# Block-causal attention into a squared-ReLU MLP: row maxima that scale the scores in PSUM, 32-bit moves of k's halves, and weight bits prepared on GpSimd

## The chip, the core and the metric

The kernel runs on one core of one Trainium2 chip. A core has five engines with a queue of instructions each: TensorE (PE in the profile, with its weight loads as PEld), VectorE (DVE), ScalarE (ACT), GpSimd (POOL) and SyncE (SP), whose queue issues the transfers between the chip's memory and SBUF. PE writes its results to PSUM, DVE and ACT read and write PSUM and SBUF, GpSimd works on SBUF. The metric is device time in microseconds, as the median of the runs; a lower time is better.

## The reference

```python
# q, k, v: 8 batches, 8 heads, 576 positions, 64 per head; blocks of 64 positions
scores = scale * np.matmul(q, k.transpose(0, 1, 3, 2))
scores = np.where(block_i >= block_j, scores, -1000000000.0)
scores = scores - np.max(scores, axis=-1, keepdims=True)
attn = np.exp(scores)
attn = attn / (np.sum(attn, axis=-1, keepdims=True) + 1e-09)
x = np.matmul(attn, v)            # then 4608 rows of 512
h = x @ w_in                      # 512 -> 2048
r = np.maximum(h, 0.0)
out = (r * r) @ w_out             # 2048 -> 512
```

The mask works on blocks: a row of block j sees the 64(j+1) positions of blocks 0 to j, so the kernel computes scores of 64 to 576 columns for the nine blocks of rows. The two weight matrices come as float64 numbers, which the kernel reads as pairs of 32-bit words.

## The kernel before, in words

**Attention passes.** Two heads are done together in a pass, one in each half of the partitions; eight batches of four pairs make 32 pairs. The first two batches are split by rows: passes 0 to 7 do row blocks 0 to 2 (G_X), passes 8 to 15 blocks 3 to 8 (G_Y). Passes 16 to 39 do all nine blocks of the other six batches (G_XY). Passes below 16 are "native": their scores are fp32 matmuls (L422). Passes below 12 are "whole": their weights are turned by PE (L515) and multiplied with fp32 v (L547). The others split every fp32 number into a high and a low fp16 part (`front`, L395 and L398 make the low parts of k and q, L402 makes `k2`, which is `k1` with its high and low halves exchanged), turn them by DMA transposes and multiply in fp16 (L433).

**Softmax of a group.** A pass has its row blocks in groups of two to four; a group's scores lie in one PSUM tile `ps` of two banks. For each block DVE takes the negated maximum of the row (L457), then one instruction multiplies the group's maxima by the scale `es` (L460), a constant in native passes and a [128, 1] tile in the others. ACT computes exp(es * score + nmx) from PSUM and its sum (L463), GpSimd adds 1e-9 to the sums (L471), DVE inverts them (L472), and ACT and DVE write the two fp16 parts of the weights, `p_rows` (L487, L488). DMA turns these (L491), PE multiplies with v (L547), ACT reads that out (L554).

**The MLP.** Its rows are taken in 12 chunks of 384 (`moe_in`, `moe_out`). A chunk is 16 hidden steps of 12 matmuls each (L683, followed by Relu on ACT L689, the square L691, and the two fp16 parts on DVE L692 and L693) and 12 output steps of 12 matmuls (L708, read out by DVE in L715). The weights are needed as two fp16 parts. `weight_scale` finds their largest value (L257), `weight_parts` makes the parts: ACT computes fp32 words from the high word of each float64 (L295), DVE shifts them by 3 (L296) and puts in the top 3 bits of the low word (L297), ACT casts to the high part (L298), DVE subtracts to get the low one (L299). w_in is loaded once, at the start (`load_w1`), into buffers that partly lie in the still unused w_out tiles; w_out is loaded twice (`load_w`, L217), for its scale and for its parts, through three buffers and eight free stretches of the w_out tiles (SPARE).

**The order of the work.** `one_pass` issues a pass; between its groups `pour` issues MLP steps, FILL[i // 4 - 2] of them in pass i, from the list of chunks that are ready. What is left when the passes end is issued after them. The first chunk goes through `first_moe`, which mixes its hidden steps with the rest of w_in's parts, w_out's scale (two pieces a step from step 2 on) and w_out's parts: PTN = 3 a step from step PT0 on, where PT0 = 16 means behind all hidden steps. The program is built with scheduling on (`schedule_with_timeline_sim`): an instruction may be placed on its engine's queue earlier or later than the code has it, as a planner finds its inputs ready, but the queues are fixed when the program runs. On PE, ACT, DVE and GpSimd an instruction that waits holds up all behind it.

Of the kernel before, what the change touches and what calls it, by code (L numbers as in the profile page):

```python
# [8 lines left out]
F32 = mybir.dt.float32  # L9
F16 = mybir.dt.float16  # L10
BF16 = mybir.dt.bfloat16
I32 = mybir.dt.int32
I64 = mybir.dt.int64
AF = mybir.ActivationFunctionType
ALU = mybir.AluOpType
AX = mybir.AxisListType
PSUM = bass.MemoryType.PSUM

P = 128
D = 64  # L20
# [9 lines left out]
A_ATT = 14  # L30
# [10 lines left out]
SC0 = 2  # L41
SCN = 2
PTN = 3
PT0 = 16
X_POOL = 1
QF = (6, 7)
WT = 1
# [1 line left out]
SPARE = {0: 2, 1: 3, 2: 4, 3: 5, 4: 6, 5: 7, 8: 6, 9: 7}  # L49
# [15 lines left out]
NW = -1  # L65
XR_ACT = 1
DELAY = (14, 6, 1)
FILL = (14, 5, 7, 7, 10, 10, 8, 7)

# [28 lines left out]
def attention_moe_kernel(ctx: ExitStack, tc: tile.TileContext, qkt, qk, vm, vt, w_in, w_out, out):  # L100
    nc = tc.nc
# [9 lines left out]

    one = const.tile([1, 1], F32, name="one")
    nc.vector.memset(one, 1.0)
    ones_bf = const.tile([P, P], BF16, name="ones_bf")
    nc.vector.memset(ones_bf, 1.0)

# [87 lines left out]
    def words(raw):  # L204

        w = raw.bitcast(I32).rearrange("p (n t) -> p n t", t=2)
        wf = raw.bitcast(F32).rearrange("p (n t) -> p n t", t=2)
        return w[:, :, 0], w[:, :, 1], wf[:, :, 1]

    def spare(k):  # L210

# [3 lines left out]
    def load_w(src, f, name, at=None):  # L215
        raw = p2.tile([P, 512], I64, tag="qk32", name=name, bufs=3) if at is None else spare(at)
        nc.sync.dma_start(raw, src[f])  # L217
        return words(raw)
# [10 lines left out]
    w1raw = []  # L229
# [5 lines left out]
    def load_w1(f, pool):  # L235


        if f in QF:
            raw = p2.tile([P, 512], I64, tag="qk32", name=f"w1raw{f}", bufs=3)
        elif f < 8:  # L240
            raw = pool.tile([P, 512], I64, name=f"w1raw{f}")
        else:
            w = (w2h, w2l)[f // 12].rearrange("p f d -> p (f d)").bitcast(I64)
            raw = w[:, f % 4 * 512 : f % 4 * 512 + 512]
        nc.sync.dma_start(raw, w_in[f])
        w1raw.append(words(raw))

    def weight_scale(wi):

        tok, ng = ((tokA, NG), (tokB, 1))[wi]
        st = small.tile([P, NF], F32, tag="stw", name=f"stw_{wi}", bufs=1)
        n = NF // ng
        for f in range(NF):
            _, _, hf = load_w(w_out, f, f"wa{wi}_{f}") if wi else w1raw[f]
            i = nc.vector.tensor_reduce(st[:, f : f + 1], hf, axis=AX.X, op=ALU.max, apply_absolute_value=True)  # L257
            if wi == 0 and f >= BS and (1, 0) in gate:
                behind(i, gate[1, 0])
            if f % n == n - 1:  # L260
                q = f // n
                st1 = small.tile([P, 1], F32, tag="st1", name=f"st1_{wi}_{q}", bufs=1)
                nc.vector.reduce_max(st1, st[:, f + 1 - n : f + 1], axis=AX.X)
                m = pow2_of_max(st1, 1, f"w{wi}_{q}", 2.0**-27, wm[:, q : q + 1] if wi == 0 else None)
                s = wsc[wi][:, q : q + 1]
                nc.vector.tensor_scalar(
                    s.bitcast(I32), m.bitcast(I32), -1, (127 + 64 + W_TOP) << 23, op0=ALU.mult, op1=ALU.add
                )
            yield
        if wi == 0:  # L270
            m = small.tile([P, 1], F32, tag="m", name="m_w")
            nc.vector.reduce_max(m, wm, axis=AX.X)
        nc.vector.tensor_scalar(
            tok.bitcast(I32), m.bitcast(I32), 8, (127 - W_EXP) << 23, op0=ALU.mult, op1=ALU.add
        )
        if wi == 0:
            nc.vector.tensor_scalar(tokA, tokA, 2.0 ** (A_X + A_W - 1), None, op0=ALU.mult)
            inv = scale_of(m, 0, 1, "w")
            nc.vector.tensor_scalar(wm, wm, inv, None, op0=ALU.mult)
            nc.vector.tensor_tensor(wm, wm, wm, op=ALU.mult)  # L280
        else:
            nc.vector.tensor_scalar(tokB, tokB, tokA, None, op0=ALU.mult)
            nc.vector.tensor_scalar(wm, wm, wsc[1], None, op0=ALU.mult)

    def weight_parts(wi):

        wh, wl = ((w1h, w1l), (w2h, w2l))[wi]
        for f in range(NF):
            wlo, whi, hf = load_w(w_out, f, f"wb{wi}_{f}", SPARE.get(f)) if wi else w1raw[f]
            if WT:  # L290
                t = p1.tile([P, 512], F32, tag=("qs", "k1", "k2")[(wi + f) % 3], name=f"wt{wi}_{f}")
            else:
                t = p2.tile([P, 512], F32, tag="r", name=f"wt{wi}_{f}", bufs=3)
            q = f * NG // NF
            nc.scalar.activation(t, hf, AF.Prelu, scale=(wm if wi else wsc[0])[:, q : q + 1], alpha=-(2.0**32))  # L295
            nc.vector.tensor_scalar(whi, t.bitcast(I32), 3, None, op0=ALU.logical_shift_left)  # L296
            nc.vector.scalar_tensor_tensor(whi, wlo, 29, whi, op0=ALU.logical_shift_right, op1=ALU.bitwise_or)  # L297
            nc.scalar.copy(wh[:, f], hf)  # L298
            nc.vector.tensor_tensor(wl[:, f], hf, wh[:, f], op=ALU.subtract)  # L299
            yield  # L300
# [3 lines left out]
    def load_first(b, hp):  # L304

        n = NHP // 2 * b + hp // 2
# [13 lines left out]
        for c in range(2):  # L320
            o = v[:, c, 0:4].rearrange("p (h n) d -> p h n d", h=2)
            nc.sync.dma_start(o, vm[b, hp + c, :, :, 0:2, :])
            passes[NHP * b + hp + c].update(
                qz=[t[:, c, h] for h in range(2)], kf=t[:, c, 2], chunks=2, v32=o, es=D**-0.5
            )

    def load(t):
# [31 lines left out]
    def front(t):  # L359

        u, c = t["u"], t["chunks"]
        if t["whole"]:
            t["es"] = D**-0.5
            return
        v32 = t["v32"][:, :, 0:c, :]
        st = small.tile([P, 3], F32, tag="st", name=f"st_{u}")
# [17 lines left out]
        nc.vector.tensor_scalar(xsc, m[:, 2 - a : 3 - a], 2.0 ** (-A_ATT - A_P), None, op0=ALU.mult)  # L384
        t["xsc"] = xsc
        if t["native"]:
            t["es"] = D**-0.5
        else:
            es = t["es"] = small.tile([P, 1], F32, tag="es", name=f"es_{u}")
            nc.vector.tensor_scalar(  # L390
                es, m[:, 0:1], m[:, 1:2], 2.0 ** (-2 * A_ATT) * D**-0.5, op0=ALU.mult, op1=ALU.mult
            )
            nc.scalar.activation(k1[:, :, 0:D], k3, AF.Copy, scale=s[:, 1:2])
            nc.scalar.activation(qs[:, :, 0:D], q3, AF.Copy, scale=s[:, 0:1])
# [3 lines left out]
            nc.vector.scalar_tensor_tensor(  # L398
                qs[:, :, D:P], q3, s[:, 0:1], qs[:, :, 0:D], op0=ALU.mult, op1=ALU.subtract
            )  # L400
            halves = k1.rearrange("p j (z d) -> p j z d", z=2)
            nc.vector.tensor_copy(k2.rearrange("p j (z d) -> p j z d", z=2), halves[:, :, ::-1, :])  # L402
            qT = t["qT"] = p2.tile([P, NJ, P], F16, tag="qT", name=f"qT_{u}")
            kT = t["kT"] = p2.tile([P, 2, NJ, P], F16, tag="kT", name=f"kT_{u}")
            nc.sync.dma_start_transpose(kT[:, 0], k1.rearrange("p j d -> p (j d)"))
# [36 lines left out]
    def softmax(t, group, complete):  # L442
# [11 lines left out]
            scores(t, ps, j, off)  # L454
        for i, (j, off) in enumerate(group):
            w = D * (j + 1)
            nc.vector.tensor_reduce(  # L457
                nmx[:, i : i + 1], ps[:, off : off + w], axis=AX.X, op=ALU.max, negate=True
            )
        nc.vector.tensor_scalar(nmx, nmx, es, None, op0=ALU.mult)  # L460
        for i, (j, off) in enumerate(group):
            w = D * (j + 1)
            nc.scalar.activation(  # L463
                p32[:, off : off + w],
                ps[:, off : off + w],
                AF.Exp,
                bias=nmx[:, i : i + 1],
                scale=es,
                accum_out=sm[:, i : i + 1],
            )  # L470
        nc.gpsimd.tensor_scalar(sm, sm, 1e-9, 2.0**-A_P, op0=ALU.add, op1=ALU.mult)  # L471
# [429 lines left out]
```

## Time and profile before

| | us |
|---|---|
| median of 3 runs | 1070.2 |
| lowest and highest of them | 1069.17 and 1070.45 |
| the profiled execution | 1070.82 |
| span of its core, first instruction to last | 1069.0 |

In the profiled execution the mean granted clock of PE is 0.981 of full speed, and the transfers move 133.08 MB at a mean of 124 GB/s.

In the rows of the profile, a group stands as: line, engine, operation, output<-input by the program's names, shapes, xcount | busy us, mean ns of one | idle us of the engine just before them <-what ended it. PE's rows are of pipelined matmuls: one row's time is longer than the distance to the next matmul, so the distance is read from start times or from a long piece of the chain. A wait row reads: who waited, for what, total us, times, longest.

### The profile page before, as it was taken

What the parts mean: (1) busy time and instruction counts of PE and PEld (TensorE: products, weight loads), DVE (VectorE), ACT (ScalarE), POOL (GpSimd) and SP (SyncE); (2) the same over time, 40 slices, a digit from 0 to 9 for tenths busy, and PEclk for the clock granted to TensorE, in tenths of its full rate; (3) what the DMA queues carried; (4) which work ended last, traced back from release to release, by engine and by line L of the source; (5) the groups of instructions that cost most, each with busy time, mean ns of one, the idle gap of its engine ahead of it and who ended that gap; (6) DMA issues with size and microseconds to landing.
All of it is one profiled execution on the core that took longest, in us unless ns stands there. A gap on an engine that the chain in (4) does not pass through costs nothing.

```text
span 1069.0 us, 18806 instructions
## 1 busy us (share of the span) xinstructions
PE 1008.9 (94%) x6836; PEld 537.2 (50%) x6836; DVE 708.9 (66%) x1859; ACT 681.2 (64%) x1668; POOL 49.5 (5%) x151
## 2 busy tenths in 40 slices
PE   6789889999988998999999999999999999999998
PEld 4345434544544454555445455455445545455553
DVE  5999787777777678968569469768967334232230
ACT  6697875885897589669559469669857315032230
POOL 2010110000000000000001000000100000000000
PEclk9799989999999998999999999999999999999999
DMA  8777259687867677769456667767574220000000
GB/s 274 260 251 270 64 169 225 121 156 151 183 136 138 139 139 152 148 133 164 116 118 129 138 134 135 147 148 129 107 142 78 31 62 1 20 11 11 21 1 29
DMA packets 303900, 133.08 MB, mean 124 GB/s; under 512 B 275648, under 2 KB 288960, under 8 KB 303808
## 3 DMA queue, kind: packets, MB, share of 16 engines
q1 hardware_dynamic: 303808, 131.90, 55.2%
q8 instruction: 53, 0.87, 0.3%
q14 instruction: 39, 0.32, 0.1%
HBM read 55.31 MB, written 9.44 MB: 61 GB/s over the span
## 4 chain that ended last, share of the span: by engine, by line
PE 60%; ACT 8%; DVE 8%; DMA 7%; issue 4%; SPq 1%; POOL 0%; ACTq 0%; DVEq 0%; POOLq 0%
PE po L708 33%; PE ph L683 19%; PE ps L433 4%; PE px L547 3%; ACT p L463 2%; ACT p_rows L487 2%; DMA kT<-k 2%; DMA p_turned<-p_rows 2%; DMA qT<-qs 2%; DVE nmx L457 2%; DVE p_rows L488 2%; ACT r L689 1%; ACT r L691 1%; DMA vraw<-in_vt 1%; DVE g L693 1%
## 5 line engine op out<-in xcount | busy, mean ns | idle before, releaser
L683 PE MATMUL ph<-xt,w1h 128*128 128x384 f16 x1536 | 378.5, 329 | 14.6 <-ACT r L689 13.7
L708 PE MATMUL po<-w2h,g 128*128 128x512 f16 x1152 | 355.3, 382 | 3.0 <-ACT w2h L298 2.0
L708 PEld LDWEIGHTS <-g 128*128 128x128 f16 x1728 | 165.7, 98 | 205.1 <-issue 17.9
L683 PE MATMUL ph<-xt,w1l 128*128 128x384 f16 x768 | 251.8, 328 | 0.0
L708 PE MATMUL po<-w2l,g 128*128 128x512 f16 x576 | 220.1, 382 | 2.2 <-DVE w2l L299 2.1
L683 PEld LDWEIGHTS <-w1h 128*128 128x128 f16 x1536 | 145.0, 98 | 122.3 <-issue 32.9
L689 ACT ACTIVATE r<-ph 128x384 f32<-128x384 f32 x192 | 93.3, 494 | 137.0 <-PE ph L683 135.4
L463 ACT ACTIVATE p<-ps,nmx,es 128x320 f32<-128x320 f32 (+8 forms) x216 | 131.6, 621 | 68.7 <-DVE nmx L460 60.4
L457 DVE TENSOR_REDUCE nmx<-ps 128x1 f32<-128x192 f32 (+8 forms) x288 | 125.4, 481 | 50.3 <-PE ps L433 40.2
L488 DVE SCALAR_TENSOR_TENSOR p_rows<-p,rs,p_rows 128x384 f16<-128x384 f32 (+4 forms) x264 | 128.0, 523 | 28.6 <-ACT p_rows L487 26.4
L487 ACT ACTIVATE p_rows<-p,rs 128x384 f16<-128x384 f32 (+4 forms) x264 | 124.6, 549 | 14.5 <-DVE rs L472 8.2
L715 DVE TENSOR_SCALAR ob<-po,uv 128x512 f32<-128x512 f32 x36 | 29.0, 807 | 122.9 <-PE po L708 122.8
L692 DVE CAST g<-r 128x384 f16<-128x384 f32 x192 | 66.9, 353 | 64.5 <-ACT r L691 64.2
L693 DVE TENSOR_TENSOR g<-r,g 128x384 f16<-128x384 f32 x192 | 104.8, 552 | 2.8
L691 ACT ACTIVATE r<-r 128x384 f32<-128x384 f32 x192 | 100.6, 531 | 2.9
L683 PEld LDWEIGHTS <-w1l 128*128 128x128 f16 x768 | 75.5, 98 | 50.5 <-issue 1.5
L433 PE MATMUL ps<-kT,qT 128*64 128x64 f16 (+6 forms) x960 | 82.4, 291 | 9.2 <-DMA qT<-qs 7.9
L547 PE MATMUL px<-p_turned,v 128*64 128x384 f16 (+5 forms) x1168 | 76.6, 271 | 4.9 <-DMA p_turned<-p_rows 2.7
L471 POOL TENSOR_SCALAR sm<-sm 128x2 f32<-128x2 f32 (+2 forms) x104 | 35.0, 336 | 727.4 <-ACT p L463 683.0
L433 PEld LDWEIGHTS <-qT 128*64 128x64 f16 x960 | 44.4, 110 | 43.5 <-issue 21.6
L547 PEld LDWEIGHTS <-v 128*64 128x64 f16 x1128 | 52.4, 110 | 26.4 <-issue 14.8
L554 ACT ACTIVATE x<-px,xsc 128x384 f32<-128x384 f32 (+1 forms) x52 | 26.2, 509 | 37.4 <-PE px L547 34.8
(134 smaller groups left out, 858.9 us busy)
## 6 DMA issues: line engine op xcount, KB each, us to landing
qk<-in_qk SPq DMA_DIRECT2D x24, 576.0 KB, 4.8
wa<-in_w_out SPq DMA_DIRECT2D x16, 512.0 KB, 5.3
out<-ob SPq DMA_DIRECT2D x32, 256.0 KB, 2.3
vraw<-in_vm SPq DMA_DIRECT2D x30, 256.0 KB, 3.6
w1raw<-in_w_in SPq DMA_DIRECT2D x8, 512.0 KB, 6.8
wb<-in_w_out SPq DMA_DIRECT2D x8, 512.0 KB, 4.3
kf<-in_qkt SPq DMA_DIRECT2D x8, 288.0 KB, 3.2
w2h<-in_w_in SPq DMA_DIRECT2D x4, 512.0 KB, 10.4
```

The costliest lines, as they stand in the source:

```text
L433: nc.tensor.matmul(ps[hs, o].rearrange("p (n d) -> p n d", d=D), t["qT"][:, j, hs], t["kT"][:, z, c0:c1, hs], start=(z == 0), stop=(z == 1),)
L457: nc.vector.tensor_reduce(nmx[:, i : i + 1], ps[:, off : off + w], axis=AX.X, op=ALU.max, negate=True)
L463: nc.scalar.activation(p32[:, off : off + w], ps[:, off : off + w], AF.Exp, bias=nmx[:, i : i + 1], scale=es, accum_out=sm[:, i : i + 1],)
L487: nc.scalar.activation(hi, p, AF.Copy, scale=rs[:, i : i + 1])
L488: nc.vector.scalar_tensor_tensor(lo, p, rs[:, i : i + 1], hi, op0=ALU.mult, op1=ALU.subtract)
L547: nc.tensor.matmul(px[hs, D * a :].rearrange("p (j d) -> p j d", d=D), lhs, rhs, start=(c == 0 and pi == 0), stop=(c == NCH[g] - 1 and (pi ...
L683: nc.tensor.matmul(ph[:, :CH], w[:, f, P * cc : P * cc + P], xt[:, z, cc, :], start=(i == 0), stop=(i == 11))
L689: nc.scalar.activation(r, ph[:, :CH], AF.Relu, scale=c)
L691: nc.scalar.activation(r, r, AF.Square)
L692: nc.vector.tensor_copy(g[:, 0], r)
L693: nc.vector.tensor_tensor(g[:, 1], r, g[:, 0], op=ALU.subtract)
L708: nc.tensor.matmul(po, gs[f][:, z, P * t : P * t + P], w[:, f, :], start=(i == 0), stop=(i == 3 * NF - 1))
```

## The change

- **Row maxima.** L457's reduce and L460's scaling are replaced by one `tensor_tensor_reduce` for each block. It computes (score + 0) * es with the negated scale, writes that back over the scores in PSUM, and gives the minimum, which is the negated scaled maximum. The zero is a [128, 1] tile read again for each column. Exp then takes scale -1.0 and the minimum as its bias. `es` is negative in all passes.
- **k's halves.** `k2` is made by a `tensor_scalar` (bitwise or with 0) over 32-bit words, half as many as the 16-bit numbers of the copy.
- **Weights.** A new function `low_bits` lets GpSimd replace the low word of each float64 by its top 3 bits: it reads the upper 16 bits of the low word, adds -4095.5 and multiplies by 2^-13, and writes an integer. It is issued behind the loads of w_in and behind the second loads of w_out. DVE's two instructions (L296, L297) become one, which shifts by 3 and puts in the prepared bits.
- **Order.** PT0 goes from 16 to 8: w_out's parts are issued from hidden step 8 on. FILL's second entry (passes 12 to 15) goes from 5 to 6, its seventh (passes 32 to 35) from 8 to 9.

```diff
-PT0 = 16
+PT0 = 8
-FILL = (14, 5, 7, 7, 10, 10, 8, 7)
+FILL = (14, 6, 7, 7, 10, 10, 9, 7)
...
+    zero = const.tile([P, 1], F32, name="zero")
+    nc.vector.memset(zero, 0.0)
...
-        return w[:, :, 0], w[:, :, 1], wf[:, :, 1]
+        return w[:, :, 0], w[:, :, 1], wf[:, :, 1], raw.bitcast(U16).rearrange("p (n t) -> p n t", t=4)[:, :, 1]
+
+    def low_bits(raw):
+        lo, _, _, top = raw
+        nc.gpsimd.tensor_scalar(lo, top, -4095.5, 2.0**-13, op0=ALU.add, op1=ALU.mult)
...
         w1raw.append(words(raw))
+        low_bits(w1raw[f])
...
-            wlo, whi, hf = load_w(w_out, f, f"wb{wi}_{f}", SPARE.get(f)) if wi else w1raw[f]
+            raw = load_w(w_out, f, f"wb{wi}_{f}", SPARE.get(f)) if wi else w1raw[f]
+            if wi:
+                low_bits(raw)
+            wlo, whi, hf, _ = raw
...
-            nc.vector.tensor_scalar(whi, t.bitcast(I32), 3, None, op0=ALU.logical_shift_left)
-            nc.vector.scalar_tensor_tensor(whi, wlo, 29, whi, op0=ALU.logical_shift_right, op1=ALU.bitwise_or)
+            nc.vector.scalar_tensor_tensor(
+                whi, t.bitcast(I32), 3, wlo, op0=ALU.logical_shift_left, op1=ALU.bitwise_or
+            )
...
-            halves = k1.rearrange("p j (z d) -> p j z d", z=2)
-            nc.vector.tensor_copy(k2.rearrange("p j (z d) -> p j z d", z=2), halves[:, :, ::-1, :])
+            pairs = [k.bitcast(I32).rearrange("p j (z d) -> p j z d", z=2) for k in (k1, k2)]
+            nc.vector.tensor_scalar(pairs[1], pairs[0][:, :, ::-1, :], 0, None, op0=ALU.bitwise_or)
...
-            nc.vector.tensor_reduce(
-                nmx[:, i : i + 1], ps[:, off : off + w], axis=AX.X, op=ALU.max, negate=True
+            nc.vector.tensor_tensor_reduce(
+                ps[:, off : off + w],
+                ps[:, off : off + w],
+                zero.to_broadcast([P, w]),
+                es,
+                3e38,
+                op0=ALU.add,
+                op1=ALU.min,
+                accum_out=nmx[:, i : i + 1],
             )
-        nc.vector.tensor_scalar(nmx, nmx, es, None, op0=ALU.mult)
...
-                scale=es,
+                scale=-1.0,
```

`es` is negated where it is set: in `load_first`, in `front` for native and whole passes (`-(D**-0.5)`), and in the instruction that multiplies it out for the others.

More of the change, by code (lines that the diff above doesn't have):

```diff
@@ L13 @@
 I64 = mybir.dt.int64
+U16 = mybir.dt.uint16
 AF = mybir.ActivationFunctionType
@@ L255, in weight_scale @@
         for f in range(NF):
-            _, _, hf = load_w(w_out, f, f"wa{wi}_{f}") if wi else w1raw[f]
+            _, _, hf, _ = load_w(w_out, f, f"wa{wi}_{f}") if wi else w1raw[f]
             i = nc.vector.tensor_reduce(st[:, f : f + 1], hf, axis=AX.X, op=ALU.max, apply_absolute_value=True)
@@ L323, in load_first @@
             passes[NHP * b + hp + c].update(
-                qz=[t[:, c, h] for h in range(2)], kf=t[:, c, 2], chunks=2, v32=o, es=D**-0.5
+                qz=[t[:, c, h] for h in range(2)], kf=t[:, c, 2], chunks=2, v32=o, es=-(D**-0.5)
             )
@@ L362, in front @@
         if t["whole"]:
-            t["es"] = D**-0.5
+            t["es"] = -(D**-0.5)
             return
@@ L386, in front @@
         if t["native"]:
-            t["es"] = D**-0.5
+            t["es"] = -(D**-0.5)
         else:
@@ L390, in front @@
             nc.vector.tensor_scalar(
-                es, m[:, 0:1], m[:, 1:2], 2.0 ** (-2 * A_ATT) * D**-0.5, op0=ALU.mult, op1=ALU.mult
+                es, m[:, 0:1], m[:, 1:2], -(2.0 ** (-2 * A_ATT)) * D**-0.5, op0=ALU.mult, op1=ALU.mult
             )
```

## The prediction

> **What bounds the kernel now.** I read the page first: shares of the engines, then the chain that ended last.
>
> ```profile
> span 1069.0 us, 18806 instructions
> ...
> PE 1008.9 (94%) x6836; PEld 537.2 (50%) x6836; DVE 708.9 (66%) x1859; ACT 681.2 (64%) x1668; POOL 49.5 (5%) x151
> ...
> PE po L708 33%; PE ph L683 19%; PE ps L433 4%; PE px L547 3%; ACT p L463 2%; ACT p_rows L487 2%; DMA kT<-k 2%; DMA p_turned<-p_rows 2%; DMA qT<-qs 2%; DVE nmx L457 2%; DVE p_rows L488 2%; ACT r L689 1%; ACT r L691 1%; DMA vraw<-in_vt 1%; DVE g L693 1%
> ```
>
> TensorE (PE) is busy 94% and carries most of the chain; what VectorE (DVE), ScalarE (ACT) and GpSimd (POOL) save counts only where PE waits for them. So the next view is busy time by stretch; the cuts are mine, where the work changes. The columns are busy us (and instructions) of PE, PEld, DVE, ACT, POOL, then granted clock, DMA share, GB/s.
>
> ```profile
> 27.00:101.00 74.00, 62.96 (x389) 35.73 (x389) 72.73 (x191) 60.19 (x138) 7.21 (x18) 0.91 0.82 278
> 101.00:140.00 39.00, 33.40 (x197) 16.25 (x196) 30.53 (x80) 32.17 (x69) 3.65 (x13) 0.96 0.28 91
> 140.00:187.00 47.00, 43.92 (x243) 19.60 (x244) 36.87 (x89) 30.12 (x65) 4.77 (x11) 0.93 0.81 188
> 187.00:500.00 313.00, 295.83 (x2229) 158.31 (x2227) 240.00 (x651) 243.73 (x619) 11.79 (x40) 0.98 0.74 146
> 500.00:830.00 330.00, 322.05 (x2324) 171.09 (x2321) 240.27 (x639) 237.92 (x601) 14.09 (x37) 1.00 0.64 128
> 878.00:1069.00 191.00, 187.03 (x1011) 98.43 (x1009) 58.03 (x119) 48.82 (x96) 0.00 (x0) 1.00 0.04 14
> ```
>
> Four regimes. From 27 to 101 us DVE is the bound: 72.73 of 74 us, while PE idles 11 us. From 101 to 187 no engine is full and PE idles 5.6 + 3.1 us. From 187 to 830 attention and MoE run mixed; PE idles 17.2 + 8.0 us in 643. From 878 on only MoE steps are left. That tail, in the chain in order of time:
>
> ```profile
> 909.39 31.08 PE po L708 x144
> 940.47 31.20 PE ph L683 x192
> ```
>
> It is PE without a gap: one chunk is 31.20 us of 16 hidden steps and 31.08 us of 12 output steps, 62.28 us for 28 steps, 2.22 us a step. Every step that is issued earlier, inside the attention, takes 2.22 us from the tail for certain, and costs in the attention what PE has no idle time for.
>
> What PE and ACT waited for between 187 and 860 us (us in total, times, longest):
>
> ```profile
> PE ph L683 <- ACT r L689: 12.5, 8, 4.0
> PE ps L433 <- DMA qT<-qs: 7.9, 6, 2.1
> ACT p L463 <- DVE nmx L460: 60.4, 21, 15.2
> ```
>
> The largest wait of PE is for PSUM that ACT's Relu has not read out; that Relu stands in ACT's queue among Exps, and ACT in turn waited 60.4 us for the scaled maxima of L460.
>
> **The change part by part. First, the tail.** In FILL, entry 1 (passes 12 to 15) goes from 5 to 6 and entry 6 (passes 32 to 35) from 8 to 9. That is one step in each of eight passes: 8 x 2.22 = -17.8 us in the tail.
>
> **Where the eight steps go.** Passes 32 to 35 lie two thirds through the 24 that fill 187 to 830, so in the stretch with PE at 322.05 of 330: nearly no room, +8.5 of their 8.9 us. Passes 12 to 15 lie in 101 to 187, where PE idles 8.7 us, 3.1 of it the stall below. I let the other 5.6 take somewhat more than half of what they could: 3.4, so +5.5 of 8.9.
>
> **Weight parts start at step 8 instead of after the hidden loop (PT0).** PE's first output work of chunk 0, and its rows where it reaches output work whose weights are not ready (start, us, idle before it and its releaser):
>
> ```profile
> 124.87 0.59 PE L708 MATMUL po<-w2h,g 128*128 128x512 f16 x2
> ...
> 140.62 0.59 PE L708 MATMUL po<-w2h,g 128*128 128x512 f16 x2 [2.04 <-ACT w2h L298]
> 143.15 0.58 PE L708 MATMUL po<-w2l,g 128*128 128x512 f16 x1 [1.10 <-DVE w2l L299]
> 143.53 1.06 PE L708 MATMUL po<-w2h,g 128*128 128x512 f16 x2
> ```
>
> That is 3.1 us of idle time. Behind it the matmuls run slow: 1.06 us for two, against 31.08 / 144 = 0.216 us each in the tail; the window's clock of 0.93 over 47 us is 3.3 us lost. Together 6.4. The parts are limited by w2's loads, of which these are the first and the last of nine, and then the rest:
>
> ```profile
> 73.55 0.43 SPq L217 DMA_DIRECT2D w2h<-in_w_out  x1
> ...
> 96.16 0.41 SPq L217 DMA_DIRECT2D wb<-in_w_out  x1
> ...
> 134.04 14.48 SPq L217 DMA_DIRECT2D wb<-in_w_out  x5
> ```
>
> Nine loads are there by about 100 us, the later ones wait until parts have freed their buffers, and the DMA share between 101 and 140 is only 0.28. If the parts run from 100 us, the later loads move past the q, k and v loads of passes 14 to 16 on SP's queue into an idle DMA, and the stall goes. What is late next there is softmax on ACT, so I count -5 of 6.4; if the planner still puts the parts behind the softmaxes, 0.
>
> **Row maxima.** Rows: the reduce (count, ns min/median/max), the scaling that goes, and for one size the reduce beside a three-operand DVE instruction that also takes a per-partition scalar:
>
> ```profile
> L457 DVE TENSOR_REDUCE nmx<-ps x288: 194/490/759, 7.0 to 820.4; 128x1 f32<-128x576 f32 x20, 128x1 f32<-128x512 f32 x20, 128x1 f32<-128x320 f32 x20, 128x1 f32<-128x192 f32 x16
> L460 DVE TENSOR_SCALAR nmx<-nmx,es x72: 186/223/231, 216.2 to 821.2; 128x4 f32<-128x4 f32 x24, 128x3 f32<-128x3 f32 x24, 128x2 f32<-128x2 f32 x24
> L460 DVE TENSOR_SCALAR nmx<-nmx x32: 146/159/257, 7.7 to 210.5; 128x2 f32<-128x2 f32 x24, 128x3 f32<-128x3 f32 x8
> ...
> L457 DVE TENSOR_REDUCE nmx<-ps 128x1 f32<-128x576 f32 x32 | 24.0, 749 | 11.2 <-PE ps L433 9.5 <-PE ps L422 1.6
> L488 DVE SCALAR_TENSOR_TENSOR p_rows<-p,rs,p_rows 128x576 f16<-128x576 f32 x28 | 22.7, 812 | 15.7 <-ACT p_rows L487 15.6
> ```
>
> L460 goes: 72 x 0.223 + 32 x 0.159 = -21.1 us of DVE. The new instruction adds a zero, scales, writes PSUM and keeps a minimum. No row shows it. Below it cannot be cheaper than the reduce, which reads the same columns; above, it may stream at half the reduce's pace: the median 0.49 less some 0.13 of fixed cost (194 ns at 64 columns to 749 at 576 is 1.08 ns a column, which leaves 0.125) makes +0.36. I take the nearest row: +63 ns (812 - 749) in the 216 whose scale is a tile, +13.6 us, and 0 in the 72 whose scale is a constant. So DVE itself hardly gains. The latency does. One group of four:
>
> ```profile
> 612.07 1.22 DVE L457 TENSOR_REDUCE nmx<-ps 128x1 f32<-128x320 f32 x4 [7.45 <-PE ps L433]
> 613.32 0.23 DVE L460 TENSOR_SCALAR nmx<-nmx,es 128x4 f32<-128x4 f32 x1
> 613.67 0.62 ACT L463 ACTIVATE p<-ps,nmx,es 128x320 f32<-128x320 f32 x1 [15.24 <-DVE nmx L460]
> ```
>
> The first Exp now needs all four maxima and L460. Afterwards it needs its own: 320 of 832 columns, 0.47 of the 1.22 us, plus 0.06, plus the 0.12 between L460's end and the Exp. It starts near 612.72, some 0.95 us earlier. If the whole tile were waited for, only 0.2 would be won. The Exp also loses its scale tile:
>
> ```profile
> L463 ACT ACTIVATE p<-ps,nmx,es 128x576 f32<-128x576 f32 x24 | 20.1, 836 | 18.7 <-DVE nmx L460 18.7
> L463 ACT ACTIVATE p<-ps,nmx 128x576 f32<-128x576 f32 x8 | 6.0, 744 | 3.7 <-DVE nmx L460 2.0 <-DVE mx L187 1.5
> ```
>
> 92 ns each, 216 times: -19.9 us of ACT. All this is latency beside PE work; on the path I credit half of PE's 12.5 us of waiting for ACT's Relu: -6. The 7.9 us for qT hang on DMA and stay.
>
> **k's halves as words.**
>
> ```profile
> L402 DVE COPY k<-k 128x1152 f16<-128x1152 f16 x24 | 17.8, 744 | 0.0
> L608 DVE TENSOR_SCALAR hb<-hb 128x384 int32<-128x384 int32 x8 | 2.8, 346 | 0.0
> L608 DVE TENSOR_SCALAR hb<-hb 128x192 int32<-128x192 int32 x8 | 2.0, 255 | 0.0
> ```
>
> 576 words at L608's 0.474 ns a word make 437 ns, 0.31 less, 7.4 us of DVE over 24; if the reversed order keeps that pace away, 744 again. The copy ends behind k1 and qs, whose transposes go ahead of k2's on SP's queue, and covers nothing of PE: 0 (with each of them on the path it would be those -7.4).
>
> **Low bits on GpSimd.** In the DVE-bound stretch the 16 shifts of w1 go (this is L296 alone); nearest rows for what GpSimd pays, and one of its own slowed:
>
> ```profile
> 27.00:101.00 74.00, 7.03 (x16) 0.91 0.82 278
> ...
> L340 POOL MEMSET qz<- 64x384 f32 x16 | 7.4, 460 | 14.0 <-PE ps L422 10.8 <-issue 2.8
> L471 POOL TENSOR_SCALAR sm<-sm 128x3 f32<-128x3 f32 x32 | 7.1, 223 | 123.2 <-ACT p L463 115.6 <-DVE g L692 7.4
> ...
> 53.75 0.91 POOL L471 TENSOR_SCALAR sm<-sm 128x2 f32<-128x2 f32 x1 [20.54 <-ACT p L463]
> ```
>
> Neighbouring rows overlap a little, so 6 us of the 7.03 come off the bound. The 16 shifts of w2 lie between 101 and 187, where DVE is busy 67.4 of 86 us: 0, or as much again if those parts should be what is late. GpSimd pays (460 - 223) / 381 = 0.62 ns a column, 0.54 us for 512; with reading, striding and converting up to three times the slope, 1.2 us. I take 0.6. The Trainium skill, GPSIMD Engine Reference, section 3.1, gives 769 ns for 512 elements; by it the term below would be 5 instead of 4. The row at 53.75, 0.91 us where three columns take 0.223, shows that GpSimd and DVE get in each other's way. By 101 us some 25 of these instructions fall (16 of w1, nine of w2). I let each hold DVE for a quarter of its time: 25 x 0.6 / 4 = +4. Each waits for its load; behind it on GpSimd's queue stand the softmax sums (L471, for which DVE's reciprocal waits) and the clearing of q's halves (L340, for which PE's scores wait). That is in the same 4; the bounds are 0 and 25 x 1.2 = 30.
>
> **Sum** against the profiled execution, 1070.8 (its span 1069.0 and 1.8 around it; the median of the runs is 1070.2): tail -17.8, steps +8.5 +5.5, weight parts -5, softmax -6, DVE-bound stretch -6 +4. That is -16.8: 1054.0, or 1053.4 from the median. I say 1054.
>
> **The rivals.** *PE has no room*: the eight steps cost all of 17.8 and the softmax gives half: -17.8 + 17.8 - 5 - 3 - 2 = -10, 1061. For it: PE is busy 97.6% from 500 to 830. Against: 25 us of idle from 187 to 830. *The idle time goes*: steps cost 7 in place of 14, the softmax wins 12, the parts 6.4: -17.8 + 7 - 12 - 6.4 - 2 = -31, 1040. For it: ACT's 60 us of waiting, the 0.98 clock from 187 to 500.
>
> *GpSimd holds up DVE* (slower): place 27 to 101 us. If each low-bits instruction blocks DVE for its whole length, the terms without the +4 make -20.8, and it decides from 20.8 / 25 = 0.83 us each; at 1.0 us it is +25, net +4: 1075. For it: the 0.91 row, and DVE's 98% there. Against: nothing shows DVE rather than GpSimd being the one that waits. The Trainium skill, SBUF — State Buffer, section Who interferes with whom, says that GpSimd and DVE share one pair of SBUF ports under an exclusive lock: whichever starts first keeps it for its whole instruction, and of DVE only instructions with two SBUF inputs or in a two-port mode need it. By that rule the reduces go free and GpSimd waits as often as DVE, so less than the 25; the 0.91 row agrees, with GpSimd as the one that waits.
>
> *The new maximum streams at half pace* (slower): L457 is 2% of the chain, 21 us; 0.36 / 0.49 more makes +15 where I have -6, and -16.8 + 6 + 15 = +4: 1075. Against: a row with two inputs and a scalar costs 8% more, not 70%.
>
> **How the numbers follow.** My forecast 0.42 (1054), no room 0.20 (1061), idle goes 0.14 (1040), GpSimd 0.10 (1075), half pace 0.06 (1075); for mixtures that cancel 0.08 (about 1070). About 0.2%, 2 us, is what a measurement can tell from no change. Faster: 0.42 + 0.20 + 0.14 = 0.76; same 0.08; slower 0.16. The range runs from 1038 to 1075: it takes in the first three cases and half the slower ones.
>
> **What would show it.** Right: the page has 72 + 32 fewer DVE instructions at the maximum, first Exps starting while later maxima run, PE output work well ahead of 124.87 us, the dense tail starting near 879 as now (878) and 17 to 18 us shorter, DVE's stretch ending some 2 us sooner. Wrong: a low-bits instruction of over 0.8 us with DVE idle behind it; maxima of over 1 us for 576 columns; a dense tail that starts over 15 us later than 878.

## The result, and the profile after

| | before | after |
|---|---|---|
| median of the runs, us | 1069.68 (4 runs) | 1060.46 (4 runs) |
| lowest and highest, us | 1067.91 and 1070.45 | 1057.87 and 1061.81 |
| span of the profiled execution, us | 1069.0 | 1057.5 |
| mean granted clock of PE | 0.981 | 0.992 |

The ratio of after to before on record is 0.9921 (the two medians give 0.9914), with a 95% interval of 0.9899 to 0.9942: the changed kernel is faster by 6 to 11 us. Line numbers in the rows of after are those of the changed kernel: L447 are the fp16 scores, L471 the new maxima, L483 Exp, L567 the product with v, L703 and L709 the hidden step and its Relu, L728 the output step.

First the page of after, its span and its engines:

```profile
span 1057.5 us, 18975 instructions
...
PE 1006.5 (95%) x6836; PEld 537.1 (51%) x6836; DVE 711.5 (67%) x2012; ACT 659.7 (62%) x1668; POOL 78.4 (7%) x183
```

ACT has lost 21.5 us of work, GpSimd has gained 28.9, DVE is where it was (708.9 before). Of the 11.5 us of span, 9.1 came out of PE's idle time (60.1 before, 51.0 now), and PE's busy time is 2.4 us less at a higher granted clock. Where, is read from the same stretches as before:

```profile
27.00:101.00 74.00, 60.94 (x359) 31.66 (x356) 67.86 (x176) 59.56 (x135) 23.23 (x38) 0.91 0.83 283
101.00:140.00 39.00, 35.56 (x210) 17.59 (x207) 27.59 (x81) 31.33 (x68) 4.03 (x13) 0.96 0.23 65
140.00:187.00 47.00, 44.36 (x254) 20.84 (x254) 37.14 (x91) 31.85 (x69) 8.94 (x18) 1.00 0.83 191
187.00:500.00 313.00, 304.87 (x2292) 163.56 (x2287) 252.65 (x744) 240.06 (x636) 11.60 (x41) 1.00 0.80 153
500.00:830.00 330.00, 320.84 (x2334) 173.84 (x2332) 237.46 (x693) 220.21 (x580) 17.72 (x35) 1.00 0.63 123
```

Most of the gain sits in one row: from 187 to 500 us PE is busy 304.87 instead of 295.83 us, at full clock. The DVE-bound start (27 to 101) has 4.9 us less of DVE and no more of PE.

The clock goes with this gain. In the profiled execution of the kernel before PE was granted half the clock in seven stretches, 41 us together; in that of the changed kernel in two, 17 us. One of the seven, behind the pause ahead of it (rows of before, columns as above):

```profile
298.90:302.30 3.40, 0.08 (x1) 0.00 (x0) 3.30 (x6) 3.40 (x7) 0.00 (x0) 1.00 0.19 39
302.30:305.70 3.40, 2.95 (x10) 1.39 (x10) 2.45 (x7) 3.40 (x10) 0.19 (x1) 0.50 1.11 206
```

PE stood idle for 3.4 us and then ran at half clock for as long. So it is with all 72 such stretches in the 14 traces of this case: in the 3.4 us ahead of each, PE was busy for 63% at most. Not every such pause is followed by one. So a long wait of PE can cost more than its own length, and an order with fewer of them can gain twice. How much of the 8.4 us (0.0079) this is stays open: among the 65 executions of the kernel before that were timed beside the experiments, a mean clock higher by 0.01 goes with some 6 us less. The four of the changed kernel have 0.988 to 0.995 where those have 0.984 on average, which by itself would make 4 to 5 us.

The end, from the chain in order of time: the last piece of the attention, its product with v, in before and in after, and then the long pieces of after that follow:

```profile
860.44 1.75 PE px L547 x26
```

```profile
863.70 1.84 PE px L567 x30
```

```profile
884.09 13.76 PE ph L703 x84
897.84 31.08 PE po L728 x144
```

Start plus length: the attention ends at 865.5 us, 3.3 us later than before (862.2). Behind it the trace of before has 576 hidden and 501 output matmuls, that of after 576 and 432: 84 steps instead of 89.75, so 5.75 output steps or 14.9 us less (191.9 us to the end instead of 206.8). That the piece at 884 us has 84 hidden matmuls where it had 156 (883.94) comes from this: the hidden steps have moved ahead into the place of those output steps. So more MLP work is done inside the attention, for 3.3 us more of its time. The waits of PE and ACT between 187 and 860 us (who for what, total us, times, longest):

```profile
PE px L567 <- DMA p_turned<-p_rows: 5.5, 8, 1.2
PE ps L447 <- DMA kT<-k: 3.0, 5, 1.0
...
PE ps L447 <- DMA qT<-qs: 1.5, 2, 1.1
PE ph L703 <- ACT r L709: 1.2, 2, 0.8
```

PE's wait for Relu went from 12.5 to 1.2 us, and the one for qT from 7.9 to 1.5, though nothing in the change makes those transposes shorter; those for p_turned and kT rose, from 1.9 and 1.3 us. That points to another order of the instructions. The changed pieces themselves, grouped by form (busy us, mean ns of one):

```profile
L471 DVE CUSTOM_DVE_ANT_0 ps<-ps,zero,es 128x576 f32<-128x576 f32 x24 | 19.7, 820 | 2.2 <-PE ps L447 2.1
L471 DVE DVE_READ_ACCUMULATOR2_ANT nmx<- 128x1 f32 x288 | 40.0, 139 | 0.0
L483 ACT ACTIVATE p<-ps,nmx 128x576 f32<-128x576 f32 x32 | 23.7, 741 | 8.2 <-DVE nmx L471 8.1
L416 DVE TENSOR_SCALAR k<-k 128x576 int32<-128x576 int32 x24 | 17.8, 743 | 0.0
L217 POOL TENSOR_SCALAR wb<-wb 128x512 int32<-128x512 uint16 x8 | 7.5, 942 | 11.6 <-DMA wb<-in_w_out 10.7 <-DVE wb L309 0.8
L217 POOL TENSOR_SCALAR w2l<-w2l 128x512 int32<-128x512 uint16 x8 | 6.8, 844 | 6.6 <-DMA w2l<-in_w_out 2.5 <-DVE p_turned L537 2.2 <-DMA w2l<-in_w_in 0.9
L217 POOL TENSOR_SCALAR w2h<-w2h 128x512 int32<-128x512 uint16 x8 | 6.5, 807 | 16.8 <-DMA w2h<-in_w_out 12.3 <-DVE stw L267 4.0 <-POOL v L364 0.3
L217 POOL TENSOR_SCALAR w1raw<-w1raw 128x512 int32<-128x512 uint16 x8 | 5.4, 674 | 6.8 <-DMA w1raw<-in_w_in 3.9 <-DMA first<-in_qkt 2.9
```

Each maximum is two instructions on DVE, the pass over the scores and a readout of 139 ns. Exp is 95 ns shorter for 576 columns. The move of k2 in words takes as long as it did in halves. And one group of four in the timeline of after (start, us):

```profile
610.02 0.56 DVE L471 CUSTOM_DVE_ANT_0 ps<-ps,zero,es 128x320 f32<-128x320 f32 x1 [4.35 <-PE ps L447]
610.50 0.14 DVE L471 DVE_READ_ACCUMULATOR2_ANT nmx<- 128x1 f32 x1
...
611.78 0.29 DVE L471 CUSTOM_DVE_ANT_0 ps<-ps,zero,es 128x64 f32<-128x64 f32 x1
611.99 0.14 DVE L471 DVE_READ_ACCUMULATOR2_ANT nmx<- 128x1 f32 x1
612.25 0.53 ACT L483 ACTIVATE p<-ps,nmx 128x320 f32<-128x320 f32 x1 [7.46 <-DVE nmx L471]
```

The first Exp starts after the last readout, not after its own: 2.23 us from the first maximum to the first Exp, where it was 1.60. That is what a wait for a whole tile looks like: `ps` and `nmx` are one tile each for the whole group. Last, ACT's first row of w_out's parts, in before and in after:

```profile
119.56 0.75 ACT L295 ACTIVATE wt<-w2h,wm 128x512 f32<-128x512 f32 x1 [0.68 <-DVE wm L283]
```

```profile
121.45 0.77 ACT L308 ACTIVATE wt<-w2h,wm 128x512 f32<-128x512 f32 x1
```

In before ACT waits there for `wm`, the factor that comes from w_out's scale. The parts start no earlier in after.

### The profile page after: what moved, and what is told of

Its sections match the earlier page's. It is cut to its first block, busy times and chain, and to the rows that moved or that the text cites. A ratio compares the mean times of both kernels' runs of the same rounds, so it can differ in the third digit from the quotient of the medians.

```text
span 1057.5 us, 18975 instructions
## 1 busy us (share of the span) xinstructions
PE 1006.5 (95%) x6836; PEld 537.1 (51%) x6836; DVE 711.5 (67%) x2012; ACT 659.7 (62%) x1668; POOL 78.4 (7%) x183
## 4 chain that ended last, share of the span: by engine, by line
PE 33%; issue 30%; DVE 9%; ACT 8%; DMA 7%; POOL 2%; POOLq 0%; ACTq 0%; DVEq 0%; SPq 0%
PE po L728 18%; PE ph L703 12%; DMA p_turned<-p_rows 3%; ACT p L483 3%; DVE ps L471 3%; ACT p_rows L507 2%; PE px L567 2%; DMA kT<-k 2%; DVE p_rows L508 2%; POOL sm L491 1%; PE ps L447 1%; DMA qT<-qs 1%; DMA wb<-in_w_out 1%; ACT r L709 1%; DVE g L713 1%
## 5 line engine op out<-in xcount | busy, mean ns | idle before, releaser
L703 PE MATMUL ph<-xt,w1h 128*128 128x384 f16 x1536 | 376.7, 327 | 2.4 <-ACT r L709 1.2
L728 PE MATMUL po<-w2h,g 128*128 128x512 f16 x1152 | 351.1, 379 | 2.9 <-ACT r L709 2.0
L728 PEld LDWEIGHTS <-g 128*128 128x128 f16 x1728 | 165.7, 98 | 199.7 <-issue 7.0
L703 PE MATMUL ph<-xt,w1l 128*128 128x384 f16 x768 | 250.2, 326 | 0.0
L728 PE MATMUL po<-w2l,g 128*128 128x512 f16 x576 | 218.0, 379 | 0.5 <-DVE w2l L313 0.5
L483 ACT ACTIVATE p<-ps,nmx 128x192 f32<-128x192 f32 (+8 forms) x288 | 148.6, 528 | 103.7 <-DVE nmx L471 91.8
L703 PEld LDWEIGHTS <-w1h 128*128 128x128 f16 x1536 | 142.6, 98 | 106.0 <-issue 16.1
L709 ACT ACTIVATE r<-ph 128x384 f32<-128x384 f32 x192 | 93.4, 490 | 122.6 <-PE ph L703 120.7
L508 DVE SCALAR_TENSOR_TENSOR p_rows<-p,rs,p_rows 128x384 f16<-128x384 f32 (+4 forms) x264 | 128.1, 522 | 21.8 <-ACT p_rows L507 17.8
L471 DVE CUSTOM_DVE_ANT_0 ps<-ps,zero,es 128x128 f32<-128x128 f32 (+8 forms) x216 | 117.5, 551 | 27.0 <-PE ps L447 25.6
L703 PEld LDWEIGHTS <-w1l 128*128 128x128 f16 x768 | 75.1, 98 | 48.9
L491 POOL TENSOR_SCALAR sm<-sm 128x2 f32<-128x2 f32 (+2 forms) x104 | 38.5, 370 | 699.2 <-ACT p L483 575.5
L447 PE MATMUL ps<-kT,qT 128*64 128x64 f16 (+6 forms) x960 | 80.8, 290 | 6.8 <-DMA kT<-k 3.0
L567 PE MATMUL px<-p_turned,v 128*64 128x64 f16 (+5 forms) x1168 | 78.4, 273 | 6.6 <-DMA p_turned<-p_rows 5.5
L567 PEld LDWEIGHTS <-v 128*64 128x64 f16 x1128 | 53.7, 110 | 32.9 <-issue 21.1
L447 PEld LDWEIGHTS <-qT 128*64 128x64 f16 x960 | 45.5, 110 | 40.9 <-issue 26.7
L483 ACT ACTIVATION_READ_ACCUMULATOR p<-ps,nmx 128x1 f32 x288 | 59.5, 206 | 0.0
```

Source lines behind the costliest of these rows:

```text
L447: nc.tensor.matmul(ps[hs, o].rearrange("p (n d) -> p n d", d=D), t["qT"][:, j, hs], t["kT"][:, z, c0:c1, hs], start=(z == 0), stop=(z == 1),)
L471: nc.vector.tensor_tensor_reduce(ps[:, off : off + w], ps[:, off : off + w], zero.to_broadcast([P, w]), es, 3e38, op0=ALU.add, op1=ALU.min ...
L483: nc.scalar.activation(p32[:, off : off + w], ps[:, off : off + w], AF.Exp, bias=nmx[:, i : i + 1], scale=-1.0, accum_out=sm[:, i : i + 1],)
L508: nc.vector.scalar_tensor_tensor(lo, p, rs[:, i : i + 1], hi, op0=ALU.mult, op1=ALU.subtract)
L567: nc.tensor.matmul(px[hs, D * a :].rearrange("p (j d) -> p j d", d=D), lhs, rhs, start=(c == 0 and pi == 0), stop=(c == NCH[g] - 1 and (pi ...
L703: nc.tensor.matmul(ph[:, :CH], w[:, f, P * cc : P * cc + P], xt[:, z, cc, :], start=(i == 0), stop=(i == 11))
```

## The experiments

All but the changed kernel itself, whose row is that of the result, were run in five rounds with the kernel before beside them. The ratios carry the verdicts, since the kernel before was not at one time in all of them (medians of 1067.43 to 1069.68 us); 0.001 is 1.07 us. const_scale, order_b_const and after_reduce leave the scale of the scores out, so they are probes of the time alone.

| kernel | median, us | ratio to before, 95% interval |
|---|---|---|
| changed kernel | 1060.46 | 0.9921 (0.9899 to 0.9942) |
| order_only | 1086.38 | 1.0160 (1.0136 to 1.0183) |
| weights_only | 1069.78 | 1.0012 (0.9994 to 1.0030) |
| maxima_only | 1059.91 | 0.9930 (0.9908 to 0.9951) |
| no_maxima | 1076.43 | 1.0087 (1.0066 to 1.0108) |
| no_order | 1072.35 | 1.0038 (1.0023 to 1.0054) |
| neg_tile | 1081.14 | 1.0121 (1.0101 to 1.0141) |
| const_scale | 1065.99 | 0.9980 (0.9964 to 0.9996) |
| pt0_only | 1075.69 | 1.0079 (1.0057 to 1.0100) |
| order_m_tile | 1068.30 | 1.0003 (0.9991 to 1.0016) |
| order_n_const | 1077.96 | 1.0097 (1.0073 to 1.0121) |
| order_b_const | 1063.41 | 0.9959 (0.9938 to 0.9981) |
| after_reduce | 1051.98 | 0.9862 (0.9829 to 0.9895) |

### The parts one by one

Theory A was the prediction's: the gain is the order, PT0 and FILL. Rival B: it is the Exp without a scale tile, which makes room on ACT.

**order_only**: the kernel before with the two constants.

```diff
-PT0 = 16
+PT0 = 8
-FILL = (14, 5, 7, 7, 10, 10, 8, 7)
+FILL = (14, 6, 7, 7, 10, 10, 9, 7)
```

> The kernel before with PT0 = 8 and the new FILL, nothing else. Theory A (the gain is the order: eight steps leave the tail and the weight stall near 140 us goes; the new maxima bring nothing, since in the changed kernel every Exp still starts after the last maximum of its group and a maximum is two DVE instructions): most of the 9 us are here, 4 to 9 us faster. Rival B (the gain comes from Exp without a scale tile, 92 ns x 216 = 20 us of ACT, which makes the room for the eight steps): alone the order has no room and is within 2 us of before.

It is 1.6% slower, which neither theory expected. The end of its attention, and PE's waits between 187 and 875 us:

```profile
891.67 1.84 PE px L547 x30
```

```profile
PE px L547 <- DMA p_turned<-p_rows: 9.2, 9, 2.0
PE ps L433 <- DMA qT<-qs: 8.2, 6, 3.1
PE ps L433 <- DMA kT<-k: 5.5, 6, 1.7
```

Behind the attention PE has the same 84 steps as in the changed kernel, 14.9 us less than before, but the attention ends at 893.5 us, 31.3 later. Half of that is the moved work itself. In the rest PE waits more for transposes: 22.9 us in these three rows, 11.9 in the kernel before, while its wait for Relu fell from 12.5 to 5.4. Theory A fell.

**weights_only**: the low bits on GpSimd and DVE's one instruction in place of two, nothing else.

```diff
...
-            nc.vector.tensor_scalar(whi, t.bitcast(I32), 3, None, op0=ALU.logical_shift_left)
-            nc.vector.scalar_tensor_tensor(whi, wlo, 29, whi, op0=ALU.logical_shift_right, op1=ALU.bitwise_or)
+            nc.vector.scalar_tensor_tensor(
+                whi, t.bitcast(I32), 3, wlo, op0=ALU.logical_shift_left, op1=ALU.bitwise_or
+            )
```

> The kernel before with the low bits on GpSimd and one DVE instruction less for each of the 32 weight blocks, nothing else. A: DVE's stretch from 27 to 101 us, the bound there, loses about 5 us, of which 1 to 4 reach the end. B: 0 to 2, since the saved time is eaten by GpSimd's 0.7 us instructions holding DVE.

No difference: 1.0012, the interval holds 1. DVE's stretch from 27 to 101 us did lose 5.5 us (67.3 in place of 72.7), but A's 1 to 4 us do not reach the end.

**maxima_only**: L457 and L460 replaced and Exp's scale -1.0, nothing else (the new maxima as above, under the change).

```diff
...
-        nc.vector.tensor_scalar(nmx, nmx, es, None, op0=ALU.mult)
...
-                scale=es,
+                scale=-1.0,
```

> The kernel before with the new maxima and Exps, nothing else. A: a group of four takes about 2.2 us from the first maximum to the first Exp against 1.6 before, so no gain: 0 to 5 us slower. B: Exps 92 ns shorter, 4 to 8 us faster.

It has the gain of the whole change, 0.9930.

**no_maxima**: the changed kernel with the reduces, the scaling and Exp's scale tile of before.

```diff
...
-                scale=-1.0,
+                scale=es,
```

> The changed kernel with the old reduces, the scaling instruction and the scale tile in Exp put back. A: as fast as the changed kernel or up to 6 us faster (1054 to 1061 us). B: the gain is lost, 1065 us or more.

0.9% slower than before. So far B fits better than A: the maxima gain. But that the order alone loses, B did not say either.

### Does B hold?

**no_order**: the changed kernel with the old constants.

```diff
-PT0 = 8
+PT0 = 16
-FILL = (14, 6, 7, 7, 10, 10, 9, 7)
+FILL = (14, 5, 7, 7, 10, 10, 8, 7)
```

> The changed kernel with the old order (PT0 = 16, FILL's entries 5 and 8): maxima, k's words and low bits stay. Theory B (the whole gain comes from the maxima, because Exp without a scale tile is 92 ns shorter and ACT gets room; the order only moves work from the tail into the attention): 1058 to 1062, the tail starting near 876 with 156 matmuls instead of near 884 with 84. Rival C (the order loses 18 us on the kernel before, but wins once ACT has room): 1065 to 1072, the changed kernel's 1060 then needs both.

It is slower than before, just past C's range. The same instructions in the new order take 0.0117 or 12.5 us less: in the traces 14.9 us less are left behind the attention, which ends 3.1 us later (865.5 against 862.4). So the order that loses 17 us with the old maxima wins 12 with the new ones. And adding weights and k2 to maxima_only costs 11.5 us, though weights_only costs nothing and k2's row is as long as before. B alone doesn't give that.

**neg_tile**: maxima_only, with Exp's -1.0 from a tile (shown against maxima_only).

```diff
+    neg = const.tile([P, 1], F32, name="neg")
+    nc.vector.memset(neg, -1.0)
...
-                scale=-1.0,
+                scale=neg,
```

> The kernel before with the new maxima alone, but Exp takes its scale of -1.0 from a [128, 1] tile instead of a constant. Theory B: the 92 ns come back (Exp of 576 columns near 836 ns in place of 741), and with them the gain goes: 1068 to 1080, above the kernel before if the longer chain of maxima then counts too. Rival D (the gain comes from the maxima's other effects, such as scores of smaller size or the two instructions per maximum spreading PSUM reads): 1058 to 1062 as with the constant.

Just above B's upper end: 0.0191 or 20.4 us above maxima_only.

**const_scale**: the kernel before with a constant in Exp.

```diff
-                scale=es,
+                scale=2.0**-20,
```

> The kernel before, its reduces and the scaling of the maxima unchanged; Exp takes a constant scale (2^-20) instead of the [128, 1] tile, so the scale of the scores inside Exp is left out of the computation. Theory B: Exp of 576 columns near 744 ns, ACT's total near 661, time 1052 to 1061: the whole gain without the new maxima, and some more since the shorter chain of the reduces stays (1.60 us from the first maximum to the first Exp in place of 2.23). Rival D (the 92 ns lie beside PE work and bring nothing): 1066 to 1072.

Exp is as short as B says, and the time falls by 2 us alone, nearly as D says. So 92 ns in each Exp are worth 2 us in one kernel and 20 in another. What these two edits also changed is the order of the instructions: the planner is told a shorter Exp and places things anew. In the traces the 404 transfers of SyncE's queue stand in another order from the 63rd on in neg_tile (against maxima_only), and from the 144th on in const_scale (against before).

**pt0_only**: the kernel before with PT0 = 8, FILL unchanged.

```diff
-PT0 = 16
+PT0 = 8
```

> The kernel before with PT0 = 8 alone, FILL unchanged. The order alone (PT0 and FILL) cost 18 us. If FILL's added steps are what costs (ACT late among more steps, PE waiting for turned weights): 1066 to 1070, or a few us faster by the stall at 140 us. If PT0 costs (the weight parts' ACT and DVE work put between softmaxes of passes 8 to 15): 1080 to 1087, and the loss lies before 187 us.

Between the two expectations: 8 us slower, and behind the attention the 89.75 steps of before are left. So of order_only's 17 us PT0 has about half, the added steps the rest, although they leave 14.9 us less behind the attention.

### The same order, another operand

To part the duration of Exp from the order that the planner makes of it, the operand is exchanged after the planner has placed everything. The order on every engine is then that of the other kernel; in the traces it is so row for row, but for a few matmuls that start at nearly the same time.

**order_m_tile**: order and instructions of maxima_only, tile put in afterwards. **order_n_const**: order of neg_tile, constant put in afterwards.

```diff
+    for f in nc.m.functions:
+        for blk in f.blocks:
+            for n, x in enumerate(blk.instructions):
+                if type(x).__name__ == "InstActivation" and x.func == AF.Exp and "ps_" in str(x.ins[0]):
...
+                    blk.instructions[n] = copy.replace(x, ins=(x.ins[0], x.ins[1], scale, x.ins[3]))
```

> The kernel with the new maxima alone (1059.9 us), its instructions in exactly the order that the planner gave it; only the scale operand of all 288 Exps is exchanged afterwards, from the constant -1.0 for a [128, 1] tile of -1.0. So nothing differs but the 92 ns of each Exp. Theory B (the 92 ns themselves are the gain): near the 1081 of the tile version that the planner ordered for itself, at least 1072. Rival E (the gain is the order that the planner finds when it is told of a shorter Exp): 1060 to 1066.

> The reverse: the order that the planner gave the version with the tile (1081.1 us), with the constant -1.0 put into the Exps afterwards, 92 ns shorter each. Theory B: 1060 to 1066, most of the 21 us back. Rival E: 1074 to 1081, the order keeps the loss.

With maxima_only and neg_tile they make a square:

| ratio to before | constant | tile | tile costs |
|---|---|---|---|
| order planned for the constant | 0.9930 | 1.0003 | 7.8 us |
| order planned for the tile | 1.0097 | 1.0121 | 2.6 us (intervals overlap) |
| the second order costs | 17.8 us | 12.6 us | |

order_n_const came out as E says, order_m_tile between the two. The larger share is the order's: rival E has most of the 20 us, B 3 to 8. The row of Exp with the tile, in order_m_tile:

```profile
L473 ACT ACTIVATE p<-ps,nmx,neg 128x576 f32<-128x576 f32 x32 | 26.6, 832 | 23.4 <-DVE nmx L461 20.7 <-DVE mx L191 2.3 <-POOL sm L481 0.3
```

That is 91 ns more than the constant's 741. The Trainium skill, ScalarE: Activation LUTs, section What ACT_TABLE_LOAD costs, says that each operand of one value per partition adds about 93 ns to an ACTIVATE; the rows agree. Where the orders differ is read from 187 to 500 us and from PE's waits between 187 and 860. First maxima_only:

```profile
187.00:500.00 313.00, 305.26 (x2318) 165.40 (x2318) 254.28 (x754) 242.50 (x639) 14.02 (x40) 1.00 0.78 153
```

```profile
PE ph L691 <- ACT r L697: 4.2, 6, 1.7
PE ps L435 <- DMA kT<-k: 3.2, 6, 1.2
PE px L555 <- DMA p_turned<-p_rows: 2.5, 5, 0.8
...
PE ps L435 <- DMA qT<-qs: 1.6, 2, 1.4
```

Then order_n_const, the same instructions with the same durations:

```profile
187.00:500.00 313.00, 291.43 (x2185) 156.27 (x2184) 240.66 (x714) 229.43 (x604) 11.32 (x38) 0.99 0.75 148
```

```profile
PE ph L693 <- ACT r L699: 8.2, 10, 2.4
PE px L557 <- DMA p_turned<-p_rows: 7.3, 8, 2.1
PE ps L437 <- DMA qT<-qs: 7.2, 6, 2.6
PE ps L437 <- DMA kT<-k: 4.3, 5, 1.7
```

PE is 13.8 us less busy in that stretch, and the four waits add up to 27.0 us in place of 11.5. The waits for transposes weigh most in it.

**order_b_const**: order and instructions of the kernel before, the constant put in afterwards in the 216 Exps with a tile, as above.

> The kernel before in its own order, reduces and scaling included, with the constant 2^-20 put into the 216 Exps that had a scale tile, so the scale of the scores inside Exp is left out of the computation. The version that the planner ordered anew for the constant took 1066.0, 2.3 us less than before. Theory B: 1055 to 1062. Rival E: 1065 to 1068, as little as the version with its own order.

Between the two: 0.0041 or 4.4 us less, so the planner's new order in const_scale seems to have given 2 us of it back (the two intervals overlap).

### What the longer maxima cost

**after_reduce**: the changed kernel in its order, every maximum exchanged for a plain reduce, and Exp's -1.0 for 2^-20.

```diff
+            if type(x).__name__ == "InstCustomDveAnt":
+                blk.instructions[n] = copy.replace(
+                    model, name=x.name, ins=(x.ins[0],), outs=(x.outs[1],), op=ALU.max, apply_absolute_value=None,
+                    negate=True, debug=x.debug, descendants=x.descendants, sync_info=x.sync_info,
+                )
...
```

> The changed kernel with every instruction in its place, but afterwards each of the 288 two-instruction maxima is exchanged for the reduce of the kernel before (749 ns for 576 columns, one instruction), and Exp takes the constant 2^-20; the scale of the scores is left out of the computation. So DVE does about 288 x 0.2 = 58 us less, and the last maximum of a group of four comes some 0.8 us sooner, in the same order. Theory F (the longer maxima lie beside PE's work, the order of the instructions and the 92 ns of the Exps make the time): 1057 to 1062, as the changed kernel. Rival G (the first Exp of a group is late by the longer maxima, and PE waits for it in the end; the longer maxima eat a gain): 1045 to 1055.

Its ratio is 0.0059 or 6.3 us below the changed kernel's, as G says (by the two medians 8.5; the two intervals just miss each other). The same group of four, its row from 187 to 500 us, and the piece that starts at 884.09 in the changed kernel:

```profile
607.26 1.60 DVE L471 TENSOR_REDUCE nmx<-ps 128x1 f32<-128x320 f32 x4 [4.91 <-PE ps L447]
608.98 0.53 ACT L483 ACTIVATE p<-ps,nmx 128x320 f32<-128x320 f32 x1 [7.52 <-DVE nmx L471]
```

```profile
187.00:500.00 313.00, 307.04 (x2312) 164.98 (x2312) 246.01 (x630) 242.66 (x641) 10.91 (x41) 1.00 0.79 152
```

```profile
878.08 13.76 PE ph L703 x84
```

The first Exp comes 1.72 us after the first maximum instead of 2.23, and the attention ends 6.0 us sooner. DVE is far from full there (246 of 313 us) and yet its longer maxima reach the end: they stand in the chain from scores to weights. DVE's total fell by 20 us (711.5 to 691.4), not by the 58 expected, since neighbouring rows overlap. after_reduce also lacks L460, so it gives the price of the new maxima against plain reduces, not against the kernel before. It is no faster version of the computation either; among the kernels that compute all of it, none was clearly below the changed one (maxima_only is equal to it).

## Why the prediction was right, and where not

The sign was right and the time of 1060.46 lies in the range, 6.5 us above the forecast of 1054.0. The sum came out near for reasons that were partly others.

- **The tail**, -17.8: measured -14.9. Not eight steps are gone from it but 5.75, and they are output steps of 2.59 us each, not of the mean 2.22. The 84 steps that are left are three whole chunks, so by the end of the attention the work that was ready had run out; for the other 2.25 nothing was left to do. pt0_only has the old tail, so this is FILL's. The prediction also began the tail at 878 us, where the attention was over at 862.2.
- **The steps' cost in the attention**, +14: it has no fixed size. With the new maxima the attention ends 3.1 us later (862.4 in no_order, 865.5 in the changed kernel), with the old ones, PT0's cost included, 31.3 later (862.2 and 893.5). The prediction took the price from PE's idle time by stretch; PE's waits point to the order of ACT's and the transposes' work around the steps.
- **Weight parts from step 8**, -5: the step that failed is that the parts run from 100 us. They need `wm`, which comes from w_out's scale. DVE writes it at 119.3 us in before, 116.9 in pt0_only, 121.1 in the changed kernel and 124.0 in no_order, and the first part starts 0.2 to 1 us behind it each time. So PT0 had nothing to bring forward, and alone it costs 8 us. PE's waits for these weights between 101 and 187 us are 4.1 us in before, 4.0 in pt0_only, 1.6 in no_order and 1.5 in the changed kernel: the stall shrank, but not by PT0. The first output work is at 130.49 us, not well ahead of 124.87.
- **Softmax**, -6: the Exp was sized well. At a fixed order its 92 ns are worth 4.4 us in the kernel before. The step that failed is the latency. It said that the first Exp starts 0.95 us earlier, since it needs only its own maximum; it starts 0.63 us later, as the wait is for the whole tile and each maximum has a second instruction, which no DVE row of before showed. At the changed kernel's order the new maxima cost 6.3 us against plain reduces. So, by the kernels in which each was measured (Exp: 3 to 8 us by the order), the new maxima and the short Exp about cancel; no run put the old pair, reduces and L460, into the changed kernel's order.
- **The new maximum's own pace**: 820 ns where 812 was expected for a tile scale, 756 where 749 was for a constant one; half pace is out. The readouts take 40 us, L460 took 21; with 13.7 us of shifts (L296) gone, DVE's total is at +2.6 us.
- **k's words**, 0: the row took the upper bound, 743 ns.
- **DVE-bound stretch**, -6 and +4: DVE lost 4.9 us there, PE gained nothing, and weights_only is at 1.0012. The low bits took 674 to 942 ns, above the 0.6 us taken and within the bounds. The Trainium skill, GPSIMD Engine Reference, section 3.1, gives 769 ns for 512 elements; the four rows lie around it, so for the duration it was nearer than my 0.6 us. Whether DVE is held for a quarter of that, no run shows. Three of the four rows are above the 0.8 us that was named as a sign of being wrong, but DVE waited for them for 2.1 us in all (its L309 on `wb`), and weights_only is not slower beyond its interval: the rival "GpSimd holds up DVE" hardly shows.
- **The rivals**: 1061 of "PE has no room" was the nearest number, but with the new maxima PE did find room for most of the moved steps.

What gives the 8.4 us then? The maxima edit at a fixed order is about even. So by subtraction, and not by a run of its own, the gain is the order's, with the clock that comes with it; the edits change the order twice: by PT0 and FILL, and by the new durations from which the planner places all instructions. That this is large enough is shown: the same instructions differ by 12.5 us (changed kernel against no_order) and by 17.8 us (maxima_only against order_n_const) in two orders. The prediction named the planner for one edit alone and had no term for it. In the second pair the mean clocks are equal (0.987), so there the clock by itself explains nothing. It stays open which placement makes the good orders good, beyond the transposes and Relu being late for PE in the bad ones; why weights and k2 added to maxima_only cost 11.5 us; and what Exps that wait only for their own maximum would be worth, which was not run.

## What to carry to other kernels

When a planner places the instructions, an edit's time is the sum of its own price and of a new order, and here the second (2 to 18 us) was mostly larger than the first (3 to 8). Measure the price with the order held still, by exchanging an operand or an instruction after planning, before crediting or blaming the edit; and tune the order's constants (here PT0 and FILL) again after each change of a duration, as their sign can flip. In the softmax read the whole chain from the first maximum to the first Exp, with the extra instruction of an accumulating operation and the tile that the wait is for: it cost time although DVE was idle a fifth of that stretch.

## What was not expected of the hardware

- The accumulating operation shows as two DVE instructions; the readout took 139 ns, 288 times.
- 576 words of 32 bits with the halves exchanged took 743 ns, as long as 1152 numbers of 16 bits (744): moving in words brought nothing in this access pattern.
- The four reduces of one group took 1.22 us in the kernel before and 1.60 us in after_reduce, 0.13 us more for each of the last three. There the exchanged instructions keep the waits of the two-instruction maxima, which is the likely reason; no row shows it.
- GpSimd's instruction of 512 elements took between 674 and 942 ns by the buffer on which it worked.
